# All opening loads on one queue, three x tiles in one transfer, half copies, and two units ahead of a fold

## The chip, the cores and the metric

The kernel runs on one core of a Trainium2 chip. The metric is the device time of one execution in microseconds (us). Before the change it was 225.01 us, the median of three runs (224.81 to 225.06).

A core has five engines that run side by side: TensorE (PE: matmuls and transposes into PSUM; PEld is its weight load), VectorE (DVE), ScalarE (ACT), GpSimd (POOL) and SyncE (SP), which here only issues transfers (DMA). Each engine works its own instructions in program order and waits on semaphores for the others.

## The reference

The input x is 2048 tokens of 512 values. It is normalised per token, and two branches of the result are added to x:

```
xn = (x - mean) / sqrt(var + 1e-5)
A:  q, k, v = split(xn @ wqkv), 32 heads of 16
    pq, pk  = q @ w_phi, k @ w_phi                       (per head, 16 x 16)
    phi(p)  = concat(softmax(p), softmax(-p))
    kv = sum over tokens of phi(pk) v;  z = sum of phi(pk)
    o  = phi(pq) kv / (phi(pq) z + 1e-6);   A = o @ wo
B:  B  = ((xn @ w_gate) * (xn @ w_up)) @ w_down          (1792 wide)
out = x + A + B
```

All data are bf16.

## The kernel before, in words

Tokens are handled in 16 tiles of 128 and in four groups of four tiles (512 tokens). Most of the time is matmuls of the B branch and of the projections. The order on TensorE, VectorE, ScalarE, GpSimd and SyncE is the order of the program: the scheduler is switched off for them (`manual_schedule`), so each engine works what the source issues to it, in that order.

Loads. `dma_x` loads a range of x tiles, `dma_cols` a range of columns of a weight. SyncE issues x tile 0, x tile 1, x tiles 2 and 3, then wk, the first 256 columns of gate and up, w_phi, the next 640 columns of gate and up, x tiles 4 to 7, the last 896 columns of gate and up, x tiles 8 to 15, w_down and wo. The load of wv is issued by ScalarE, behind its first activation in the program (line 96), which is there to load the table for Exp. A token's row of x is 1 KB; a partition's rows of neighbouring tiles are contiguous, so tiles 1 to 3 together are 3 KB per partition.

Normalisation of the first four tiles. On VectorE, for each tile n: `ln_sums` (bn_stats, L146), then `first_apply(n - 1)` (L162), which normalises the tile before, then bn_aggr (L338) and the add of epsilon (L155); GpSimd raises it to the power -0.5 (L157). The last application follows the loop. So tile 0 is normalised only after the statistics of tile 1. Later groups are normalised by `ln_block`, which puts pieces of work ("chores") on a list; they are taken from the list at places set in the program. Their application runs on ScalarE, and their transposes are DMAs from SyncE.

Transposes of the first tiles. `lt(n)` transposes a normalised tile in four matmuls against the identity (L207) and copies the result from PSUM to xnT on ScalarE (L208). `vproj(n)` is the projection with wv in four matmuls (L235), two before and two after the call given as `amid`, by which the next tile's `lt` comes into its middle; the copy to vt is on ScalarE for tile 0, on VectorE for tiles 1 to 3.

wk. w_phi acts on k directly after the projection, so both are folded to one matrix W1k: `wk_transposes(jp)` transposes half of wk (L222) and copies it on ScalarE (L223), `make_bd` spreads w_phi over a block-diagonal on GpSimd (L214), and `fold` multiplies them (L229) and copies to W1k on ScalarE (L231). `kproj(n)` uses W1k and needs all of it.

Units. `ffn(1)` is one unit of the B branch: 128 of the 1792 columns for one group of 512 tokens. It has four gate matmuls (L272), four up matmuls (L276), a copy of gate on ScalarE (L279) and the product on VectorE (L280). There are 56 units, 14 per group; the first one needs the transposes of all four first tiles, and columns 0 to 127 of gate and up.

`warm_up(k)` issues k matmuls on zeros, whose result nobody reads: ten at the start and two between `lt(0)` and `vproj(0)`. PSUM results go through a ring of six banks (`bank`).

Of the kernel before, what the change touches and what calls it, by code (L numbers as in the profile page):

```python
# [9 lines left out]
F32 = mybir.dt.float32  # L10
AF = mybir.ActivationFunctionType
ALU = mybir.AluOpType
# [9 lines left out]
def kernel(  # L22
# [12 lines left out]
    nc = tc.nc  # L35
    P = 128
    S, D = A_x.shape[-2], A_x.shape[-1]
# [4 lines left out]
    DC = D // P  # L42
    FC = F // P
    EPS = 1e-5
    GT = 4
# [12 lines left out]
    wv = wpool.tile([P, DC, D], BF16)  # L58
# [10 lines left out]
    def dma_x(lo, hi):  # L69
        nc.sync.dma_start(out=xall[:, lo:hi, :], in_=x_view[:, lo:hi, :])  # L70

    def dma_cols(eng, w, src, lo, hi, at=0):
        eng.dma_start(out=w[:, :, lo - at:hi - at], in_=src[:, lo:hi].rearrange("(c p) f -> p c f", p=P))

    F1, F2 = 2 * P, 7 * P
    for lo, hi in ((0, 1), (1, 2), (2, 4)):
        dma_x(lo, hi)
    dma_cols(nc.sync, wk, A_wqkv, D, 2 * D, at=D)
    dma_cols(nc.sync, wg, B_w_gate, 0, F1)
    dma_cols(nc.sync, wu, B_w_up, 0, F1)  # L80
# [13 lines left out]
    nc.vector.memset(zeros[:], 0.0)  # L94
    first = consts.tile([P, 1], BF16)
    nc.scalar.activation(out=first[:], in_=zeros[:, 0:1], func=AF.Exp, scale=1.0)
    dma_cols(nc.scalar, wv, A_wqkv, 2 * D, 3 * D, at=2 * D)
    ident = consts.tile([P, P], BF16)
    make_identity(nc, ident[:])
    mhalf = consts.tile([P, GT], F32)  # L100
# [15 lines left out]
    xnT = xpool.tile([P, DC, S], BF16)  # L116
# [16 lines left out]
    lnpool = ctx.enter_context(tc.tile_pool(name="ln", bufs=2))  # L133
# [16 lines left out]
        stats = ln_sums(n)  # L150
        nc.vector.bn_aggr(out=mv, in_=stats[:])

    def ln_rstd(mv, k):
        ve = lnpool.tile([P, GT], F32, name="ve")
        nc.vector.tensor_scalar(out=ve[:, 0:k], in0=mv[:, 0:k, 1], scalar1=EPS, scalar2=None, op0=ALU.add)  # L155
        rstd = lnpool.tile([P, GT], F32, name="rstd", bufs=GT)
        nc.gpsimd.tensor_tensor(out=rstd[:, 0:k], in0=ve[:, 0:k], in1=mhalf[:, 0:k], op=ALU.pow)  # L157
        return rstd
# [18 lines left out]
    def ln_block(lo):  # L177
        mv = mv_tile()
        nb = lnpool.tile([P, GT], F32, name="nb", bufs=GT)
        rstd = []  # L180

        def scales():
            ve = lnpool.tile([P, GT], F32, name="ve4")
            nc.gpsimd.tensor_scalar(out=ve[:], in0=mv[:, :, 1], scalar1=EPS, scalar2=None, op0=ALU.add)
            r = lnpool.tile([P, GT], F32, name="rstd4", bufs=GT)
            nc.gpsimd.tensor_tensor(out=r[:], in0=ve[:], in1=mhalf[:], op=ALU.pow)
            nm = lnpool.tile([P, GT], F32, name="nm")
            nc.gpsimd.tensor_scalar(out=nm[:], in0=mv[:, :, 0], scalar1=-1.0, scalar2=None, op0=ALU.mult)
            nc.gpsimd.tensor_tensor(out=nb[:], in0=nm[:], in1=r[:], op=ALU.mult)
            rstd.append(r)  # L190

        def apply(i):
            xn = xnpool.tile([P, D], BF16, name="xn")
            nc.scalar.activation(out=xn[:], in_=xall[:, lo + i, :], func=AF.Identity,
                                 scale=rstd[0][:, i:i + 1], bias=nb[:, i:i + 1])
            nc.sync.dma_start(out=xnT[:, :, (lo + i) * P:(lo + i + 1) * P], in_=xn[:], transpose=True)

        for i in range(GT):
            chores.append(lambda i=i: ln_stats(lo + i, mv[:, i, :]))
        chores.append(scales)  # L200
        for i in range(GT):
            chores.append(lambda i=i: apply(i))

    def lt(n):
        tp = bank("tp", BF16).rearrange("p (c t) -> p c t", c=DC)
        for c in range(DC):
            nc.tensor.transpose(out=tp[:, c, :], in_=xns[n][:, c * P:(c + 1) * P], identity=ident[:])  # L207
        nc.scalar.copy(out=xnT[:, :, n * P:(n + 1) * P], in_=tp)  # L208

    bd = consts.tile([P, DC, 8, DH], BF16)  # L210

# [51 lines left out]
    def ffn(k):  # L263
        for _ in range(k):
            if not units:
                return
            T, f = units.pop(0)
            if f == 0:
                hTs[T] = hpool.tile([P, FC, TT], BF16, name="hT", tag="h")
            gps = bank("g")  # L270
            for c in range(DC):
                nc.tensor.matmul(gps, lhsT=wg[:, c, f * P:(f + 1) * P], rhs=xnT[:, c, T * TT:(T + 1) * TT],  # L272
                                 start=(c == 0), stop=(c == DC - 1))
            ups = bank("u")
            for c in range(DC):
                nc.tensor.matmul(ups, lhsT=wu[:, c, f * P:(f + 1) * P], rhs=xnT[:, c, T * TT:(T + 1) * TT],  # L276
                                 start=(c == 0), stop=(c == DC - 1))
            g_sb = gpool.tile([P, TT], BF16, name="g_sb")
            nc.scalar.copy(out=g_sb[:], in_=gps)  # L279
            nc.vector.tensor_tensor(out=hTs[T][:, f, :], in0=ups, in1=g_sb[:], op=ALU.mult)  # L280
# [19 lines left out]
    def warm_up(k):  # L300
        for _ in range(k):
            nc.tensor.matmul(warm, lhsT=zeros[:, 0:P], rhs=zeros[:], start=True, stop=True)
# [3 lines left out]
    with tc.tile_pool(name="ps_k", bufs=1, space=PSUM) as ps_k:  # L306
        kvps = [ps_k.tile([P, 4, 4, E1], F32, name=f"kv{b}") for b in range(2)]
        phiks = {}

        def vproj(n, copy=nc.scalar.copy, amid=None):  # L310
            ps = bank("pv")
            proj(ps, n, wv, range(2))
            if amid is not None:
                amid()
            proj(ps, n, wv, range(2, DC))
            copy(out=vts[n % NV][:, :, :, 0:DH], in_=ps.rearrange("p (a b c) -> p a b c", a=8, b=4))  # L316

        def kproj(n):
            phiks[n] = features(n, W1k, "k")

        def kv(n):
            vt, phik = vts[n % NV], phiks[n]
            for gr in range(NG):
                nc.tensor.matmul(kvps[gr // 4][:, gr % 4, :, :].rearrange("p a b -> p (a b)"),  # L324
                                 lhsT=phik[:, gr, :], rhs=vt[:, gr, :, :].rearrange("p a b -> p (a b)"),
                                 start=(n == 0 and gr % 4 == 0), stop=(n == NT - 1 and gr % 4 == 3))

        mvs = [mv_tile() for n in range(GT)]
        rstds = []

        def first_apply(n):
            ln_apply(n, mvs[n][:, 0, 0:1], rstds[n][:, 0:1])

        for n in range(GT):
            stats = ln_sums(n)
            if n > 0:
                first_apply(n - 1)
            nc.vector.bn_aggr(out=mvs[n][:, 0, :], in_=stats[:])  # L338
            rstds.append(ln_rstd(mvs[n], 1))
        first_apply(GT - 1)  # L340
        make_bd()
        nc.gpsimd.tensor_tensor(out=M4[:], in0=BO[:, 0:4, :], in1=BO[:, 4:8, :], op=ALU.add)
        lt(0)
        warm_up(2)
        vproj(0, amid=lambda: lt(1))
        vproj(1, copy=nc.vector.tensor_copy, amid=lambda: lt(2))
        wk_transposes(0)
        vproj(2, copy=nc.vector.tensor_copy, amid=lambda: lt(3))
        wk_transposes(1)
        vproj(3, copy=nc.vector.tensor_copy)  # L350
        ffn(1)
        fold(1, W1k, (0, 1))
        ffn(1)
        fold(1, W1k, (2, 3))
        ffn(1)
        ln_block(4)
        ffn(1)
        chore(2)
        kproj(0)
        ffn(1)  # L360
        chore(2)
        ffn(1)
        chore()
        kproj(1)
        ffn(1)
        chore()
        ffn(1)
        kproj(2)
        chore()
        ffn(1)  # L370
        kv(0)
        chore()
        ffn(1)
        kproj(3)
        chore()
        ffn(1)
        kv(1)
        ffn(1)
        nc.sync.dma_start(out=wT2[:, 0, :, :], in_=A_wqkv[:, 0:D], transpose=True)
        for n in range(GT, NT):  # L380
            if n in (4, 8):
                ln_block(n + 4)
            vproj(n)
            kproj(n)
            chore(1 if n % GT < 2 else 0)
            ffn(1)
            kv(n - 2)
            chore((1, 2, 2, 2)[n % GT])
            if n >= 8 and n % 2 == 0:
                qproj((n - 8) // 2)  # L390
            if n == 6:
                fold(0, W1q, (0, 1))
            ffn(1)
            if n == 6:
                fold(0, W1q, (2, 3))
        ffn(1)
        kv(NT - 2)
        ffn(1)
        kv(NT - 1)
        for b in range(2):  # L400
            nc.vector.tensor_tensor(out=KV[:, 4 * b:4 * b + 4, :, :], in0=kvps[b][:],
                                    in1=_bcast_ap(M4[:], [M4[:].ap[0], [0, 4], [E1, 4], [1, E1]]), op=ALU.mult)
        qproj(4)
        ffn(1)
# [64 lines left out]
```

## Time and profile before

| what | value |
|---|---|
| median of three runs | 225.01 us |
| the profiled execution | 224.9 us |
| its span, first to last instruction | 223.2 us |
| TensorE busy | 217.4 us (97%) |
| VectorE busy | 137.9 us (62%) |
| ScalarE busy | 90.3 us (40%) |
| GpSimd busy | 72.1 us (32%) |
| moved by DMA | 19.91 MB, mean 89 GB/s |

The profile is one execution. Times in its views count from the first instruction. The chain of waits follows what ended last backwards, at each step to what released it; its lines give the start, the length and the engine with the line of the program. A line of the timeline gives the start, the length, the engine and line, the operation with what it writes and reads, how often it is repeated there, and in square brackets how long the engine was idle before it and what released it. A line for a load gives the issuing queue, how many there are, the size of each and the median time from issue to landing. An idle engine costs nothing unless the chain runs through it.

### The profile page before, as it was taken

Reading aid. Unit: us, or ns where it says so; the run is one execution under the profiler, and the core shown is the slowest. Engines: PE = TensorE matmul, PEld = TensorE weight load, DVE = VectorE, ACT = ScalarE, POOL = GpSimd, SP = SyncE. Lnnn points to the kernel's source line nnn. Section 1 sums busy time; section 2 is a strip of 40 time slices with the busy share of each in tenths; the row PEclk is TensorE's granted clock in tenths of the full one; section 3 lists DMA queues with packets and bytes.
Section 4 is the critical chain, followed back from the end, with each engine's and each line's share of the span. In section 5 each row is a group of like instructions: output and inputs, shape, how many; then the busy total and the mean of one; then the engine's idle time right before and its main releaser. Section 6 shows DMA issues by size and latency. Waiting matters only on the chain.

```text
span 223.2 us, 3437 instructions
## 1 busy us (share of the span) xinstructions
PE 217.4 (97%) x1278; PEld 105.4 (47%) x1278; DVE 137.9 (62%) x237; ACT 90.3 (40%) x161; POOL 72.1 (32%) x59
## 2 busy tenths in 40 slices
PE   7799999999999999999999999999999999999994
PEld 2354444445444444444454444444444444444453
DVE  5634986586559875757679975097745746444321
ACT  2574575448955685646354122222222222100000
POOL 3310455336235663636315453014033033000000
PEclk9999999999999999999999999999999999999999
DMA  6999923501110224020203664314431431622301
GB/s 178 317 381 394 349 55 74 94 1 21 38 38 0 47 50 94 1 47 3 47 1 71 99 140 94 75 24 94 94 73 24 93 72 24 91 55 71 72 25 47
DMA packets 44481, 19.91 MB, mean 89 GB/s; under 512 B 35248, under 2 KB 44080, under 8 KB 44336
## 3 DMA queue, kind: packets, MB, share of 16 engines
q1 hardware_dynamic: 43936, 19.16, 34.8%
q10 hardware_dynamic: 528, 0.52, 0.8%
q8 instruction: 10, 0.16, 0.3%
q14 instruction: 7, 0.06, 0.1%
HBM read 9.19 MB, written 2.10 MB: 51 GB/s over the span
## 4 chain that ended last, share of the span: by engine, by line
PE 95%; DMA 2%; DVE 1%; SPq 0%; ACT 0%; issue 0%
PE fin L288 22%; PE u L276 22%; PE g L272 22%; PE fin L291 6%; PE k L235 6%; PE q L235 6%; PE pv L235 6%; DMA xall<-in_A_x_dram 2%; PE ab L412 2%; PE kv L324 2%; PE pq L229 1%; PE tp L222 0%; PE tp L207 0%; SPq L70 0%; DVE stats L146 0%; ACT xnT L208 0%
## 5 line engine op out<-in xcount | busy, mean ns | idle before, releaser
L276 PE MATMUL u<-xnT,wu 128*128 128x512 bf16 x224 | 57.5, 379 | 0.0
L272 PE MATMUL g<-xnT,wg 128*128 128x512 bf16 x224 | 57.5, 379 | 0.0
L280 DVE TENSOR_TENSOR hT<-u,g_sb 128x512 bf16<-128x512 f32 x56 | 37.1, 668 | 28.3 <-PE u L276 19.5
L247 DVE TENSOR_REDUCE sums<-e 128x64 f32<-128x1024 f32 x32 | 38.9, 1215 | 21.5 <-ACT e L244 21.5
L279 ACT CAST g_sb<-g 128x512 bf16<-128x512 f32 x56 | 32.9, 588 | 46.5 <-PE g L272 46.5
L288 PE MATMUL fin<-wd,hT 128*128 128x512 bf16 (+1 forms) x238 | 51.1, 366 | 0.0
L251 POOL TENSOR_TENSOR phiq<-e,rs 128x1024 bf16<-128x1024 f32 x16 | 30.9, 1932 | 61.5 <-DVE rs L249 53.2
L251 POOL TENSOR_TENSOR phik<-e,rs 128x1024 bf16<-128x1024 f32 x16 | 30.9, 1932 | 47.6 <-DVE rs L249 45.6
L276 PEld LDWEIGHTS <-wu 128*128 128x128 bf16 x224 | 21.9, 98 | 26.4
L288 PEld LDWEIGHTS <-hT 128*128 128x128 bf16 x238 | 23.0, 98 | 24.1
L272 PEld LDWEIGHTS <-wg 128*128 128x128 bf16 x224 | 21.1, 98 | 23.4
L235 PEld LDWEIGHTS <-xnT 128*128 128x128 bf16 x192 | 17.2, 97 | 18.7 <-ACT xnT L208 1.7
L294 DVE TENSOR_TENSOR o_sb<-fin,xall 128x512 bf16<-128x512 f32 (+1 forms) x17 | 11.2, 656 | 22.4 <-PE fin L291 22.4
L243 ACT ACTIVATE e<-q 128x512 f32<-128x512 f32 x16 | 9.5, 596 | 26.1 <-PE q L235 26.1
L249 DVE RECIPROCAL rs<-sums 128x64 f32<-128x64 f32 x32 | 17.7, 553 | 3.1
L235 PE MATMUL pv<-wv,xnT 128*128 128x512 bf16 x64 | 16.9, 379 | 0.6 <-ACT xnT L208 0.5
L291 PE MATMUL fin<-wo,oT 128*128 128x512 bf16 (+1 forms) x68 | 16.6, 366 | 0.0
L235 PE MATMUL k<-W1k,xnT 128*128 128x512 bf16 x64 | 16.4, 379 | 0.0
L235 PE MATMUL q<-W1q,xnT 128*128 128x512 bf16 x64 | 16.4, 378 | 0.0
L243 ACT ACTIVATE e<-k 128x512 f32<-128x512 f32 x16 | 9.6, 597 | 7.0 <-PE k L235 7.0
L316 ACT CAST vt<-pv 128x512 bf16<-128x512 f32 x13 | 7.7, 591 | 11.5 <-PE pv L235 11.5
L146 DVE BATCH_NORM_STATS2 stats<-xall 128x6 f32<-128x512 bf16 x16 | 10.7, 670 | 2.2 <-DMA xall<-in_A_x_dram 2.2
(50 smaller groups left out, 125.1 us busy)
## 6 DMA issues: line engine op xcount, KB each, us to landing
out_dram<-o_sb SPq DMA_DIRECT2D x15, 128.0 KB, 1.9
wd<-in_B_w_down_dram SPq DMA_DIRECT2D x1, 1792.0 KB, 17.5
xall<-in_A_x_dram SPq DMA_DIRECT2D x1, 1024.0 KB, 13.4
wg<-in_B_w_gate_dram SPq DMA_DIRECT2D x1, 896.0 KB, 8.5
wu<-in_B_w_up_dram SPq DMA_DIRECT2D x1, 896.0 KB, 11.4
wg<-in_B_w_gate_dram SPq DMA_DIRECT2D x1, 640.0 KB, 7.9
wu<-in_B_w_up_dram SPq DMA_DIRECT2D x1, 640.0 KB, 7.0
wv<-in_A_wqkv_dram ACTq DMA_DIRECT2D x1, 512.0 KB, 4.4
```

What stands on the lines that cost most here:

```text
L235: nc.tensor.matmul(ps, lhsT=xnT[:, j, n * P:(n + 1) * P], rhs=w[:, j, :], start=(j == 0), stop=(j == DC - 1))
L243: nc.scalar.activation(out=e[:, :, 0, :], in_=pfv, func=AF.Exp, scale=1.0)
L247: nc.vector.tensor_reduce(out=sums[:], in_=ev, axis=AX.X, op=ALU.add)
L249: nc.vector.reciprocal(out=rs[:].rearrange("p a b -> p (a b)"), in_=sums[:])
L251: nc.gpsimd.tensor_tensor(out=phi[:].rearrange("p g (x f) -> p (g x) f", f=DH), in0=ev, in1=rs[:].to_broadcast((P, 2 * H, DH)), op=ALU.mult)
L272: nc.tensor.matmul(gps, lhsT=wg[:, c, f * P:(f + 1) * P], rhs=xnT[:, c, T * TT:(T + 1) * TT], start=(c == 0), stop=(c == DC - 1))
L276: nc.tensor.matmul(ups, lhsT=wu[:, c, f * P:(f + 1) * P], rhs=xnT[:, c, T * TT:(T + 1) * TT], start=(c == 0), stop=(c == DC - 1))
L279: nc.scalar.copy(out=g_sb[:], in_=gps)
L280: nc.vector.tensor_tensor(out=hTs[T][:, f, :], in0=ups, in1=g_sb[:], op=ALU.mult)
L288: nc.tensor.matmul(ps, lhsT=hTs[T][:, f, t4 * P:(t4 + 1) * P], rhs=wd[:, f, lo:lo + w], start=(f == 0), stop=False)
L291: nc.tensor.matmul(ps, lhsT=oTs[n][:, c, :], rhs=wo[:, c, lo:lo + w], start=False, stop=(c == DC - 1))
L294: nc.vector.tensor_tensor(out=o_sb[:], in0=ps, in1=xall[:, n, lo:lo + w], op=ALU.add)
```

## The change

The loads of the opening are all issued by SyncE, in this order: x tile 0; x tiles 1 to 3 in one transfer; wv; then wk and the rest as before. ScalarE issues none. The copies of the transposes of tiles 0 and 1 are made in two halves of two column blocks each. The two warm-up matmuls between `lt(0)` and `vproj(0)` are left out; the ten at the start stay. In front of the first fold stand two units instead of one, between the folds one as before, and after the second fold one instead of two, so that four stand in front of the first k projection as before. `ln_rstd` takes the engine of its add as an argument and serves the later groups too; the instructions and their engines are the same, but the later groups now share the buffers `ve` and `rstd` with the first tiles.

```diff
     F1, F2 = 2 * P, 7 * P
-    for lo, hi in ((0, 1), (1, 2), (2, 4)):
-        dma_x(lo, hi)
+    dma_x(0, 1)
+    dma_x(1, 4)
+    dma_cols(nc.sync, wv, A_wqkv, 2 * D, 3 * D, at=2 * D)
     dma_cols(nc.sync, wk, A_wqkv, D, 2 * D, at=D)
...
     nc.scalar.activation(out=first[:], in_=zeros[:, 0:1], func=AF.Exp, scale=1.0)
-    dma_cols(nc.scalar, wv, A_wqkv, 2 * D, 3 * D, at=2 * D)
...
-    def ln_rstd(mv, k):
+    def ln_rstd(eng, mv, k):
         ve = lnpool.tile([P, GT], F32, name="ve")
-        nc.vector.tensor_scalar(out=ve[:, 0:k], in0=mv[:, 0:k, 1], scalar1=EPS, scalar2=None, op0=ALU.add)
+        eng.tensor_scalar(out=ve[:, 0:k], in0=mv[:, 0:k, 1], scalar1=EPS, scalar2=None, op0=ALU.add)
...
         def scales():
-            ve = lnpool.tile([P, GT], F32, name="ve4")
-            nc.gpsimd.tensor_scalar(out=ve[:], in0=mv[:, :, 1], scalar1=EPS, scalar2=None, op0=ALU.add)
-            r = lnpool.tile([P, GT], F32, name="rstd4", bufs=GT)
-            nc.gpsimd.tensor_tensor(out=r[:], in0=ve[:], in1=mhalf[:], op=ALU.pow)
+            r = ln_rstd(nc.gpsimd, mv, GT)
...
-    def lt(n):
+    def lt(n, parts=1):
         tp = bank("tp", BF16).rearrange("p (c t) -> p c t", c=DC)
         for c in range(DC):
             nc.tensor.transpose(out=tp[:, c, :], in_=xns[n][:, c * P:(c + 1) * P], identity=ident[:])
-        nc.scalar.copy(out=xnT[:, :, n * P:(n + 1) * P], in_=tp)
+        for c in range(0, DC, DC // parts):
+            nc.scalar.copy(out=xnT[:, c:c + DC // parts, n * P:(n + 1) * P], in_=tp[:, c:c + DC // parts, :])
...
-            rstds.append(ln_rstd(mvs[n], 1))
+            rstds.append(ln_rstd(nc.vector, mvs[n], 1))
...
-        lt(0)
-        warm_up(2)
-        vproj(0, amid=lambda: lt(1))
+        lt(0, parts=2)
+        vproj(0, amid=lambda: lt(1, parts=2))
...
-        ffn(1)
+        ffn(2)
         fold(1, W1k, (0, 1))
         ffn(1)
         fold(1, W1k, (2, 3))
-        ffn(1)
         ln_block(4)
         ffn(1)
         chore(2)
```

## The prediction

> **What bounds the kernel now.** I read the page's busy line and chain summary first, then the chain of waits for the first 16 us, then the timeline of the same stretch, then the loads.
>
> ```profile
> PE 217.4 (97%) x1278; PEld 105.4 (47%) x1278; DVE 137.9 (62%) x237; ACT 90.3 (40%) x161; POOL 72.1 (32%) x59
> ...
> PE 95%; DMA 2%; DVE 1%; SPq 0%; ACT 0%; issue 0%
> ```
>
> TensorE is busy 97% of the span and carries 95% of the chain. What is left sits in the opening and in the short tail. From the first unit on, pieces of TensorE follow each other without a hole (the eight matmuls of a unit take 2 x 0.86 us), so an opening that ends earlier by some amount ends the kernel earlier by that amount. The chain in the opening (columns: start, length, what):
>
> ```profile
> 1.71 4.88 DMA xall<-in_A_x_dram
> 6.59 0.02 issue
> 6.61 0.69 DVE stats L146
> 7.31 0.33 DVE xn L162
> 7.63 0.05 issue
> 7.68 0.41 PE tp L207 x4
> 8.09 0.02 issue
> 8.11 0.59 ACT xnT L208
> 8.71 0.05 issue
> 8.75 0.60 PE pv L235 x2
> 9.36 0.22 PE tp L207 x4
> ...
> 12.05 1.04 PE pv L235 x4
> 13.09 0.86 PE g L272 x4
> ```
>
> One transfer, x tiles 2 and 3 together, lands at 6.59. Behind it VectorE takes tile 2's statistics, only then applies tile 1's normalisation, and TensorE can transpose tile 1. From 8.75 TensorE is nearly gapless up to the first unit at 13.09: 4.34 us. So the opening is set by a load, by VectorE's order, and by one ScalarE copy. The timeline, same stretch:
>
> ```profile
> 1.22 0.46 ACTq L73 DMA_DIRECT2D wv<-in_A_wqkv_dram  x1
> ...
> 2.99 0.69 DVE L146 BATCH_NORM_STATS2 stats<-xall 128x6 f32<-128x512 bf16 x1 [1.11 <-DMA xall<-in_A_x_dram]
> ...
> 4.01 0.68 DVE L146 BATCH_NORM_STATS2 stats<-xall 128x6 f32<-128x512 bf16 x1
> ...
> 7.22 0.40 DVE L162 TENSOR_SCALAR xn<-xall,mv,rstd 128x512 bf16<-128x512 bf16 x1
> ...
> 8.56 0.41 DVE L162 TENSOR_SCALAR xn<-xall,mv,rstd 128x512 bf16<-128x512 bf16 x1
> ```
>
> And the loads (last column: us from issue to landing):
>
> ```profile
> wv<-in_A_wqkv_dram ACTq DMA_DIRECT2D x1, 512.0 KB, 4.4
> wk<-in_A_wqkv_dram SPq DMA_DIRECT2D x1, 512.0 KB, 6.3
> xall<-in_A_x_dram SPq DMA_DIRECT2D x2, 128.0 KB, 2.3
> xall<-in_A_x_dram SPq DMA_DIRECT2D x1, 256.0 KB, 4.9
> ```
>
> wv, issued on ScalarE's queue at 1.22, landed at 5.62. The 256 KB of x, issued at 1.71, came after it although they are half as large: in this trace a load goes by its issue time over both queues, and wv stood in front of tiles 2 and 3.
>
> **The change, part by part.** I write L for the landing of x tiles 1 to 3 and V for that of wv.
>
> Issue slots. SP issues x tile 0 at 0.79, the next at 1.25, the third at 1.71, wk at 2.18. Afterwards tiles 1 to 3 have the second slot, wv the third (each 0.40 to 0.46 us), and wk keeps 2.18. ScalarE loses an issue of 0.46 us that lay beside its table load (0.78 to 2.06): nothing gained. wk and all behind it have the same 1024 KB in front as before, so I leave their landings: wk 2.18 + 6.3 = 8.5, gate 9.35, up 10.4, w_phi 10.7, and so on. wv's 512 KB now stand in SP's queue too, and SP's own stall (a 2.64 us issue at 4.45) may begin sooner; the loads it holds have margins, given below.
>
> L. Issue at 1.25. Before, 256 KB of x had landed by 1.25 + 2.3 = 3.55, and 768 KB (x 0, x 1, wv) by 5.62. Tiles 0 to 3 are 512 KB, half-way: 4.6. From below, VectorE is busy with tile 0 until about 4.0, so landing before that is worth nothing more. From above, L's 384 KB are no slower than wv's 512 KB, 4.4 us from issue: 5.65. I take the half-way value, 4.6: it comes from loads of the same stretch on both sides.
>
> The fit of the Trainium skill ("DMA: Bandwidth & Descriptors", section "Anatomy of one DMA — SWDGE (gpsimd) path") is 2.0 us plus bytes at 436 GB/s, stated for loads that GpSimd issues; it gives an estimate of 1.25 + 2.0 + 0.9 = 4.15 for L. It fits the 128 KB loads here (2.3 us) and fails for the 256 KB one (4.9 us against 2.6), which had others in front. By it, and by L alone, the end would be 0.45 us earlier than by the rows, 223.7 us; I stay with the rows.
>
> V. With wv last of the same 1024 KB: 768 KB at 5.62, 1024 KB at 6.59 before. That is the value for no faster transfer, and 1.71 + 4.4 = 6.1 the one for its own time from issue. I take 6.4, a little nearer to the first, which counts bytes.
>
> VectorE's path. The new wait: tile 1's statistics started at 4.01 without waiting, now at L + 0.02, and the application of tile 0, which is queued behind them, with them. Before, 6.61 to 7.22 is statistics to application (0.61), and two applications stand 1.34 us apart (7.22, 8.56). So tile 0 is applied at L + 0.63 = 5.23 instead of 4.79 (0.44 us late), tile 1 at L + 1.97 = 6.57 instead of 7.22, tile 2 at L + 3.31 = 7.91 instead of 8.56. There are now three tiles behind the late landing instead of two: 1.34 us of the 1.99 us by which the landing is earlier (6.59 - 4.6) are spent again.
>
> Tile 1 to the first unit. Application 0.41 and 0.05 issue, transposes 0.41, 0.02, then the copy. A whole copy (128x512) is 0.586 us and one of 128x1024 is 1.012: 0.426 per 512 columns on 0.16 fixed, so a half is 0.37, an estimate between 0.20 (the 128x1 activation at 2.08) and 0.586. The first two matmuls read the first half alone: 0.22 us gained. 0.05 more, and tile 1's wv matmuls start at L + 1.97 + 0.46 + 0.43 + 0.37 + 0.05 = L + 3.28. Two halves take 0.74 instead of 0.586 on ScalarE; the second half is read only after the next tile's transposes, which hide that 0.16. From these matmuls to the first unit, 4.34 us as before: L + 7.62. Tile 2's transposes there begin 0.61 after, L + 3.89, and tile 2 is ready at L + 3.31 + 0.41 + 0.05 = L + 3.77: hidden, with 0.1 to spare. With L = 4.6 the first unit starts at 12.22, not 13.09: 0.87 earlier.
>
> The other input. The first wv matmuls start at V + 0.05, and tile 0's first half is there at 5.23 + 0.46 + 0.43 + 0.37 + 0.05 = 6.54, so with V = 6.4 neither waits on the other. By V alone: 0.43 for two matmuls, 0.41 tile 1's transposes, 0.44 half copy with its two hand-overs, then 4.34: V + 5.67 = 12.07, short of 12.22. Both inputs limit within 0.15 us.
>
> Two warm-up matmuls go (0.59 us busy from 5.49): before, the wv matmuls behind them started at 6.33, released by the copy, so nothing was lost to them and nothing is won. What they covered was a hole of TensorE; the holes now are from 5.14 to 5.7 and from 6.1 to 6.54, no longer than the 0.74 before 7.68, across which the page's slices show a granted clock of nine tenths or more. I cost it at 0; if the clock fell, see the rivals.
>
> Two units in front of the fold. Same matmuls, other order; before, TensorE had no hole from first unit to the first k projection (13.09 to 20.89 is four units of 1.73 and two folds of 0.45), so at best 0. What it costs if cover fails: gate and up's second part land at 12.4 and 14.1, wanted by the third unit at 12.22 + 3.45 + 0.45 = 16.1; w_phi's product with the mask is done at 11.86, wanted at 15.6; the last W1k copy ends 1.5 us after its fold starts (14.65 to 16.15), while one unit and the fold, 2.18, stand before the k projection. wk lands 8.5, wanted at L + 3.89 + 0.22 + 0.43 = 9.1: the thinnest margin, 0.6. The helper that now serves both normalisations issues the same GpSimd instructions; the buffers shared were read long before: 0.
>
> Sum. The opening ends 0.87 earlier, everything else is 0. The profiled execution took 224.9 with a span of 223.2 (1.7 around it), 0.1 under the median 225.01. Its forecast is 224.0, the median's 224.1.
>
> **The rivals.**
>
> Tiles 1 to 3 late, slower. All of tile 0's work now hangs on the 384 KB. Break-even is L + 7.62 = 13.09, L = 5.47, and from there each us costs one. The bound from wv's row, 5.65, gives 225.2; the 4.9 us of the 256 KB row, counted from 1.25, is L = 6.15 and 225.7. For it: the trace moved 197 to 252 GB/s in the half-us slices from 2.0 to 3.5 us, against 351 to 366 from 10 to 12 us. Against: in the 4.9 us row wv stood in front, and it no longer does.
>
> wv late. V + 5.67 = 13.09 is V = 7.42: no gain. For it: wv is now last of 1024 KB. At 6.59 the gain is 0.83 and only from 6.97 on is it under 0.45. Time 224.6 to 225.0.
>
> The gain is given back. One of the margins above fails (wk's 0.6, or the W1k copies' 0.7) or the clock falls where the warm-up stood, and the first k projection stands where it stood: 225.0. Against: the loads behind have the same bytes ahead of them. A clock at half over the whole gapless stretch (3.3 us of TensorE work from 8.75 to 12.05) would double that and make 226.5; no row hints at it.
>
> **How the numbers follow.** Forecast, gain over 0.45: 0.74. wv late: 0.12, of which 0.02 still faster. Given back: 0.04, within 0.2% (0.45 us, about what a measurement of this kernel can tell from no change), and 0.01 for the clock, slower. Tiles 1 to 3 late: 0.09, slower. So faster 0.76, no change 0.14, slower 0.10. Range: downward, L at 4.0 and V at its present 5.62 would start the first unit at 11.6, gain 1.5: 223.5; I end at 223.6. Upward to the no-gain cases and a little of the late landing: 225.1.
>
> **What would show it.** Right: the second statistics start near 4.6, waiting for x; tile 1's wv matmuls near 7.9; the first unit near 12.2 and the first k projection near 20.0, with no hole between; half copies of 0.37; GpSimd's w_phi product still near 11. Wrong: statistics after 5.4, wv's first matmuls waiting for a DMA past 6.9, a hole in front of wk's transposes, or matmuls at twice their pitch after 5 us.

## The result: slower in the median, and in two groups

With the change, the kernel takes 226.21 us (median of 20 executions, 224.63 to 226.86) against 225.05 us before (median of 20, 224.81 to 225.45). The ratio of the two is 1.0037, with a 95% interval of 1.0023 to 1.0050: slower, where I had forecast 224.1.

The executions do not scatter evenly. Seven took 224.63 to 225.18, thirteen 225.96 to 226.86, and none lies between. Of the thirteen, ten have a mean granted TensorE clock of 0.992, the others and all seven of the lower group 1.000. The profiled execution of the change is one of the upper group: 226.68 us, span 224.9. Its page has the granted clock in 40 slices:

```profile
PEclk9799999999999999999999999999999999999999
```

The second slice, 5.6 to 11.2 us, holds 7 tenths where the kernel before had 9. The chain of waits of the changed kernel for the first 20 us (start, length, what), against the one shown of before:

```profile
1.25 4.46 DMA xall<-in_A_x_dram
5.71 0.02 issue
5.73 0.69 DVE stats L146
6.43 0.32 DVE xn L162
6.75 0.05 issue
6.80 0.41 PE tp L204 x4
7.21 0.02 issue
7.23 0.38 ACT xnT L206
7.61 0.04 issue
7.66 0.61 PE pv L233 x2
8.26 0.30 PE tp L204 x4
8.56 1.71 PE pv L233 x4
10.27 0.43 PE tp L204 x4
...
14.83 0.86 PE g L270 x4
```

The first unit (line g) starts at 14.83; before it was 13.09. That is 1.74 later, and the profiled executions differ by 226.68 - 224.9 = 1.78, so all but 0.04 us of the loss is in the opening. Two things stand in these lines. x tiles 1 to 3 land at 5.71, not at the 4.6 that I had taken. And from 8.43 on the matmuls take twice their time: four wv matmuls 1.71 us where two took 0.43, four transposes 0.43 instead of 0.22. The loads of the changed kernel (last column: us from issue to landing):

```profile
wv<-in_A_wqkv_dram SPq DMA_DIRECT2D x1, 512.0 KB, 5.6
wk<-in_A_wqkv_dram SPq DMA_DIRECT2D x1, 512.0 KB, 6.6
...
xall<-in_A_x_dram SPq DMA_DIRECT2D x1, 384.0 KB, 4.5
```

wv, issued at 1.71, lands at 7.3 instead of 6.4. The clock can be read from the busy time by stretches (columns: stretch, its length, then the busy time and the number of instructions of TensorE, its weight load, VectorE, ScalarE and GpSimd, then granted clock, DMA share, GB/s). First the changed kernel, from the instant at which its clock was raised (the records of the clock begin there):

```profile
5.02:8.43 3.41, 1.57 (x13) 0.61 (x12) 2.55 (x9) 0.65 (x2) 0.56 (x1) 1.00 1.08 348
8.43:11.85 3.42, 3.42 (x18) 1.73 (x16) 1.89 (x6) 1.82 (x4) 1.88 (x3) 0.50 1.12 307
```

and the kernel before, from the rise of the clock in its own trace:

```profile
4.45:7.86 3.41, 2.30 (x15) 0.73 (x14) 2.11 (x9) 0.59 (x1) 0.86 (x2) 1.00 0.99 322
```

In the changed kernel TensorE worked 1.57 us in the 3.41 us after the rise, and for the next 3.41 us the clock was 0.50. Before it worked 2.30 us, and the clock stayed.

By my own path, L + 7.62 with L = 5.71 gives 13.33: 0.24 of the 1.74 us is the landing, and the other 1.50 us I put down to the clock. The row of the fallen clock allows that much: 3.42 us of TensorE work at half the clock are 1.71 us at the full one.

### The profile page after: what moved, and what is told of

Its sections match the earlier page's. It is cut to its first block, busy times and chain, and to the rows that moved or that the text cites. A ratio compares the mean times of both kernels' runs of the same rounds, so it can differ in the third digit from the quotient of the medians.

```text
span 224.9 us, 3411 instructions
## 1 busy us (share of the span) xinstructions
PE 217.4 (97%) x1252; PEld 106.1 (47%) x1276; DVE 137.9 (61%) x237; ACT 90.6 (40%) x163; POOL 72.2 (32%) x59
## 4 chain that ended last, share of the span: by engine, by line
PE 95%; DMA 2%; issue 1%; DVE 1%; SPq 0%; ACT 0%
PE g L270 22%; PE u L274 21%; PE fin L286 21%; PE pv L233 7%; PE fin L289 6%; PE k L233 6%; PE q L233 6%; DMA xall<-in_A_x_dram 2%; PE kv L322 2%; PE ab L408 2%; PE pq L227 1%; PE tp L204 1%; PE tp L220 0%; DVE stats L146 0%; DVE o_sb L292 0%
## 5 line engine op out<-in xcount | busy, mean ns | idle before, releaser
L292 DVE TENSOR_TENSOR o_sb<-fin,xall 128x512 bf16<-128x512 f32 (+1 forms) x17 | 11.2, 656 | 22.4 <-PE fin L289 21.5
L233 PE MATMUL pv<-wv,xnT 128*128 128x512 bf16 x61 | 17.8, 404 | 0.6 <-ACT xnT L206 0.5
```

What stands on the lines that cost most here:

```text
L233: nc.tensor.matmul(ps, lhsT=xnT[:, j, n * P:(n + 1) * P], rhs=w[:, j, :], start=(j == 0), stop=(j == DC - 1))
L292: nc.vector.tensor_tensor(out=o_sb[:], in0=ps, in1=xall[:, n, lo:lo + w], op=ALU.add)
```

## The experiments

Two theories to begin with. Clock theory: the late landing and the two missing warm-ups leave TensorE with too little work after the ten warm-ups, and the clock falls. Landing theory: the late x tiles are the whole loss. All kernels were compared with the kernel before on the same chip, whose medians were 224.99 to 225.12 there. A hole is a time in which TensorE is idle.

**Warm-ups put back.** In the changed kernel:

```diff
         lt(0, parts=2)
+        warm_up(2)
         vproj(0, amid=lambda: lt(1, parts=2))
```

> The changed kernel with the two warm-up matmuls put back in front of tile 0's wv projection. In the profile of the changed kernel TensorE worked for about 1.6 us of the 3.4 us from 5.0 to 8.4, and the granted clock then fell to 0.50 for 3.4 us. Clock theory (too little TensorE work after the ten warm-ups lets the clock fall): the two add about 0.4 us there; if that is enough the clock stays at 1.00 and every execution takes 224.6 to 225.2; if not, the times scatter as before. Landing theory (the late landing of x tiles 1 to 3 is the whole loss): 226.2 as with the change, whatever the clock does.

225.04 us (224.74 to 226.42, 12 executions), ratio 0.9998 [0.9986, 1.0011]. Ten executions took 224.74 to 225.13, two 226.34 and 226.42. So the two matmuls bring most executions back, though x still lands late (5.41 in the profiled one): the landing is not the whole loss. The profiled execution was one of the two. Its clock did not fall after a rise, it rose late, only at 10.45. Chain of waits of this kernel:

```profile
6.50 0.61 PE tp L204 x4
7.10 0.85 PE warm L300 x2
7.96 0.85 PE pv L233 x2
8.81 0.43 PE tp L204 x4
9.24 1.53 PE pv L233 x4
10.76 0.22 PE tp L204 x4
```

Transposes at 0.43 for four until 10.45, at 0.22 afterwards. The mean clock of this execution is given as 1.000 all the same, since the records begin with the rise; that may be why three slow executions of the change have 1.000 too.

**Sixteen warm-ups at the start instead of ten.**

```diff
-    warm_up(10)
+    warm_up(16)
```

> The changed kernel with sixteen warm-ups at the start instead of ten, which end at about 6.5 at the full clock's pitch, before tile 0's transposes at 6.8, so that they delay nothing. Clock theory: no fall of the clock, first unit near 13.1 instead of 14.8, 224.7 to 225.1, no execution near 226.5. Landing theory: 226.2, since x tiles 1 to 3 still land at 5.7.

225.41 us (224.84 to 225.91), 1.0007 [0.9998, 1.0016]. No execution near 226.5: the clock theory's main point holds. But the time is above the expected 224.7 to 225.1. The chain of waits says why:

```profile
1.24 6.21 PE warm L300 x16
7.45 0.24 PE tp L204 x4
```

The clock rose only at 6.51 here, the warm-ups before it had half the pace, and tile 0's transposes, whose input was there at about 6.3 (x landed at 5.24), waited for the last of them until 7.3. I had priced all six additional ones at the full pace.

**x tile 1 in a transfer of its own.**

```diff
-    dma_x(0, 1)
-    dma_x(1, 4)
+    for lo, hi in ((0, 1), (1, 2), (2, 4)):
+        dma_x(lo, hi)
```

> The changed kernel with x tile 1 and x tiles 2 and 3 loaded in two transfers again, wv behind them on SyncE. Landing theory: tile 1 lands near 3.6, tile 0 is applied at 4.8, tiles 2 and 3 land near 4.6 and wv near 6.5; then wv limits, first unit near 12.2, 224.2. Clock theory alone: the hole of TensorE after the warm-ups is shorter (tile 0's transposes at 5.2), work from 5.0 to 8.4 is over 2 us, the clock stays at 1.00 and the time is 224.2 to 224.9. If one transfer of 3 KB rows lands no later than two, the time is that of the change, 224.6 to 226.9.

225.60 us, 1.0012 [0.9987, 1.0038]: unclear, as the times again fall in two groups, five of 224.29 to 224.66 and one of 225.19, six of 226.01 to 227.25. Tile 1 landed at 3.63 and tile 0 was transposed at 5.37, as expected; but tiles 2 and 3 landed at 5.45 instead of 4.6, and wv took TensorE's place as the one waited for:

```profile
2.18 5.44 DMA wv<-in_A_wqkv_dram
7.62 0.04 issue
7.66 1.01 PE pv L233 x2
```

TensorE was idle for 1.90 us in front of wv, worked 1.34 us in the 3.42 us after the rise of the clock (3.94 to 7.36), and the clock fell. Both parts of what I expected of the clock were wrong for this run: work there was not over 2 us, since I had put wv at 6.5. The five of the lower group, 0.5 to 0.8 us under the kernel before, show what the early tile is worth where the clock holds. And 512 KB of x are down at 5.45 in two transfers as at 5.2 to 5.7 in one: the one large transfer is not what makes them late.

**wv back on ScalarE's queue.**

```diff
-    dma_cols(nc.sync, wv, A_wqkv, 2 * D, 3 * D, at=2 * D)
...
     nc.scalar.activation(out=first[:], in_=zeros[:, 0:1], func=AF.Exp, scale=1.0)
+    dma_cols(nc.scalar, wv, A_wqkv, 2 * D, 3 * D, at=2 * D)
```

> The changed kernel with wv issued by ScalarE again, at 1.22, beside x tiles 1 to 3 at 1.25. If loads go by their issue time over both queues, wv lands near 5.6 and x tiles 1 to 3 near 6.6 or later: 0.9 us later than with the change, first unit near 14 at the full clock, and a still longer hole on TensorE, so a fallen clock in most executions: 226 to 227.5. If the two queues share, x lands near 5.7 and the time is that of the change, 224.6 to 226.9.

227.00 us (225.84 to 227.93), 1.0080 [1.0059, 1.0100], inside the first expectation's range of times, but not by its mechanism: x tiles 1 to 3 landed at 6.17 and wv after them at 7.76. So two loads issued together on two queues need not land as those of before did, where I had read an order by issue time. The long hole in front of tile 0 was there (TensorE 1.43 us in the 3.41 us from 5.75), and the clock fell.

**The kernel before without its two warm-ups.**

```diff
         lt(0)
-        warm_up(2)
         vproj(0, amid=lambda: lt(1))
```

> The kernel before without the two warm-up matmuls between tile 0's transposes and its wv projection, all else as before. The granted clock goes by stretches of 3.4 us: stretches with 1.34, 1.43 and 1.57 us of TensorE work were followed by a clock of 0.50 (three kernels with x tiles 1 to 3 or wv late), one with 2.30 us was not (the kernel before). Without the two, the one of the kernel before holds about 1.9. Clock theory: if 1.9 is enough, 225.05 in every execution, the two matmuls alone are not the cause and the longer hole in front of tile 0 is; if not, a part of the executions stands 1.2 to 1.8 above, near 226.5. As I predicted it: 225.05 always.

225.04 us (224.87 to 226.26), 1.0010 [0.9998, 1.0023]. Nine executions of 12 took 224.87 to 225.14, three 225.94 to 226.26. The profiled one is of the three:

```profile
4.33:7.74 3.41, 1.75 (x10) 0.46 (x8) 1.86 (x6) 0.59 (x1) 0.97 (x2) 1.00 1.02 317
7.74:11.15 3.41, 3.20 (x14) 1.57 (x15) 2.06 (x8) 1.59 (x3) 1.56 (x3) 0.50 1.13 306
```

So the kernel before stands near the edge: without 0.43 us of useless work, a quarter of its executions fall into an upper group, and the one of them that was profiled lost its clock. One of the 29 executions of the kernel before itself on this chip took 226.04 too; it was not profiled. With the change it is thirteen of twenty, with a longer hole in front of tile 0.

**Two transfers for x and four warm-ups.** The changed kernel with x tile 1 by itself, as above, and `warm_up(4)` between `lt(0, parts=2)` and `vproj(0, ...)`.

> The changed kernel with x tile 1 and x tiles 2 and 3 in two transfers, wv behind them on SyncE, and four warm-ups between tile 0's transposes and its wv projection, where TensorE waits for wv. Clock theory: no executions near 226.3; all take what the undisturbed ones of the same loads without warm-ups took, 224.3 to 224.7. If the scatter comes from the loads and not from the clock, it stays: 224.3 to 227.2. If wv is early the four cost up to 0.4: 224.8.

224.78 us, 0.9989 [0.9977, 1.0001]; ten executions of 224.48 to 225.09 and one of 225.84. With the same loads the upper group is gone but for that one execution, which was not profiled: the scatter came with the clock and not with the loads. The time is 0.1 above what was expected; in the profiled execution the four began just before the rise of the clock at 6.21 and ended at 7.09, where wv had landed (7.05).

**wv on SyncE in the kernel before.**

```diff
-    for lo, hi in ((0, 1), (1, 2), (2, 4)):
-        dma_x(lo, hi)
+    dma_x(0, 1)
+    dma_x(1, 2)
+    dma_cols(nc.sync, wv, A_wqkv, 2 * D, 3 * D, at=2 * D)
+    dma_x(2, 4)
...
-    dma_cols(nc.scalar, wv, A_wqkv, 2 * D, 3 * D, at=2 * D)
```

> The kernel before with wv issued by SyncE, between x tile 1 and x tiles 2 and 3, so that the order of the loads is the one in which they landed before; everything else as before, the two warm-ups too. If only the order of issue counts (as I predicted), x tiles 2 and 3 land at 6.6 and the time is 225.05. If loads of one queue are served more slowly in the first microseconds than the same loads on two queues, x tiles 2 and 3 land at 7.0 to 7.6 as the last of 1024 KB did with all on SyncE: 225.5 to 226.1.

226.03 us (225.65 to 226.30), 1.0044 [1.0031, 1.0057], in one group. The order of landing is that of the kernel before, and still x tiles 2 and 3 are a microsecond later:

```profile
2.18 5.57 DMA xall<-in_A_x_dram
7.75 0.02 issue
7.77 0.69 DVE stats L147
```

So the same order and the same bytes in front did not bring the same landing. Of the 1.16 us between the two profiled executions 0.47 is the issue, 2.18 instead of 1.71; from there to landing it took 5.6 us instead of 4.9. In the profiled executions of the other kernels with the loads of before it took 5.2 to 5.5, so between 0.1 and 0.7 us are left to the one queue.

This trace also narrows down what makes the clock fall. The late tile left a hole of 1.41 us, longer than the change's 1.38, and the clock held, with 1.96 us of TensorE work in the second stretch after its rise at 4.21:

```profile
8.84 0.40 PE L208 MATMUL tp<-ident,xn 128*128 128x128 bf16 x4 [1.41 <-DVE xn L163]
...
7.62:11.04 3.42, 1.96 (x15) 0.99 (x16) 2.51 (x8) 1.34 (x3) 1.10 (x2) 1.00 1.14 312
```

In the kernel before without its two warm-ups the longest hole up to the fall was 1.02 us, and yet the clock fell. So the longest hole does not tell the two cases apart; the sum of the work in a stretch does, with the limit between 1.75 and 1.96 us of 3.41 in these two traces.

**Two queues, x first.** From the kernel with four warm-ups:

```diff
-    def dma_x(lo, hi):
-        nc.sync.dma_start(out=xall[:, lo:hi, :], in_=x_view[:, lo:hi, :])
+    def dma_x(lo, hi, eng=nc.sync):
+        eng.dma_start(out=xall[:, lo:hi, :], in_=x_view[:, lo:hi, :])
...
-    for lo, hi in ((0, 1), (1, 2), (2, 4)):
-        dma_x(lo, hi)
-    dma_cols(nc.sync, wv, A_wqkv, 2 * D, 3 * D, at=2 * D)
+    dma_x(0, 1)
+    dma_x(1, 2, nc.scalar)
+    dma_x(2, 4)
+    dma_cols(nc.scalar, wv, A_wqkv, 2 * D, 3 * D, at=2 * D)
```

> The changed kernel with the opening loads on two queues in another order: SyncE issues x tile 0, then x tiles 2 and 3, ScalarE x tile 1, then wv; and four warm-ups between tile 0's transposes and its wv projection. Queue theory (two queues are served faster in the first microseconds than one): x tile 1 lands near 3.5, x tiles 2 and 3 near 4.6, wv near 6.2, 0.9 earlier than with all on SyncE; first unit near 12, 223.9 to 224.3, and the clock does not fall. If the bytes alone count, wv lands near 7.0 as the last of 1024 KB does on one queue, and the time is that of the same kernel with all on SyncE, 224.5 to 225.1. If ScalarE's early issue delays its table load, no loss: its first copy is at 6.

225.09 us (224.92 to 225.27), 1.0002 [0.9993, 1.0011]. The queue theory falls: wv landed at 7.7 (6.5 us from its issue at 1.22), later than the 7.05 on one queue, and tile 0 itself only at 3.92 instead of 3.06:

```profile
0.79 3.13 DMA xall<-in_A_x_dram
3.92 0.02 issue
3.94 0.70 DVE stats L147
```

Tile 1 was issued beside tile 0 here, but that this made tile 0 late is not shown: in two kernels with the loads of before tile 0 landed at 3.7 and 3.8 as well.

What the late kernels had in common was then x itself: 512 KB of x are down at 5.2 or later in all of them, whatever queue and whatever size of transfer. That led to the next one.

**The halves alone, and the units in front of the fold alone**, each put into the kernel before as the change has it.

> The kernel before with the copies of tiles 0 and 1 in halves alone. Half a copy took 0.38 in the profile of the changed kernel, a whole one 0.59 before: tile 1's wv matmuls start 0.2 earlier, 8.55 instead of 8.75, and the first unit with them: 224.85. If the second half's later end holds something up: 225.05. TensorE's work in the stretch after the warm-ups stays the same, so no fall of the clock.

> The kernel before with two units in front of wk's first fold, one between the folds and one behind, as in the change, and nothing else. TensorE had no hole there before, and the margins that I counted (0.7 us for W1k, over 2 us for the loads) hold: 225.05, within 0.1. If W1k's copies come too late for the first k projection, or a transfer is wanted too early: 225.3 to 226.

Halves: 224.92 us, 0.9995 [0.9987, 1.0004], no more than 0.1 gained and not told from nothing. Units first: 225.07 us, 1.0003 [0.9994, 1.0012], nothing, as predicted.

**Another numbering of the tokens.** A tile was every sixteenth token; here it is 128 neighbours, for the input and the output alike, so that its rows lie together in memory.

```diff
-    x_view = A_x.flatten_outer_dims().rearrange("(p n) d -> p n d", n=NT)
-    out_view = out.flatten_outer_dims().rearrange("(p n) d -> p n d", n=NT)
+    x_view = A_x.flatten_outer_dims().rearrange("(n p) d -> p n d", n=NT)
+    out_view = out.flatten_outer_dims().rearrange("(n p) d -> p n d", n=NT)
```

First in the changed kernel with its two warm-ups put back, then in the one with two x transfers and four warm-ups:

> The changed kernel with the two warm-ups put back, and with another numbering of the tokens: a tile is 128 neighbouring tokens, for x and for the output, so a tile's 128 KB lie together in memory instead of 1 KB out of every 16 KB. The result is the same. Stride theory: x tiles 1 to 3 land at 5.2 to 5.7 in four kernels because rows 16 KB apart are read slowly; now they land near 4.6, where the count of bytes put them, and the executions that keep their clock take 224.0 to 224.4 instead of 224.7 to 225.1. Start theory (everything is slow in the first microseconds of loading, whatever it reads): 5.2 to 5.7 again and 224.7 to 225.1. If rows of 1 KB instead of 3 KB cost more than the stride: later than 5.7, 225.2 and more.

> The kernel with x tile 1 and x tiles 2 and 3 in two transfers, wv behind them on SyncE and four warm-ups in front of the wv projection, with the same other numbering of the tokens. Its time before was 224.78 (224.48 to 225.1 but for one). Stride theory: wv, which limits it, lands near 6.5 instead of 7.05, 224.1 to 224.5. Start theory: wv lands at 7.0 again and 224.5 to 225.1.

224.28 us (224.07 to 224.44), 0.9964 [0.9952, 0.9976], and 224.11 us (223.67 to 224.68), 0.9961 [0.9949, 0.9974]: both clearly under the kernel before, both times as the stride theory has it. Loads of the first of the two:

```profile
wv<-in_A_wqkv_dram SPq DMA_DIRECT2D x1, 512.0 KB, 4.6
...
xall<-in_A_x_dram SPq DMA_DIRECT2D x1, 384.0 KB, 3.3
```

The 384 KB land at 4.56 instead of 5.41, wv at 6.3 instead of 7.0; they are the same bytes, now in rows of 1 KB. In the second kernel wv lands at 6.63 instead of 7.05, tile 1 at 3.21 instead of 3.70, but tiles 2 and 3 only 0.14 earlier (5.12 and 5.26), which the stride theory does not explain. The landings are compared by one execution each.

Two questions were left: does the numbering act elsewhere in the kernel, and is the fall of the clock the late landing's doing, or that of the two missing warm-ups? So it was put into the kernel before alone, and into the change as it stands.

> The kernel before with the other numbering of the tokens (a tile's 128 KB together in memory) and nothing else. If the numbering acts through the landing of the first x tiles alone: x tiles 2 and 3 land a little earlier, 6.2 to 6.5 instead of 6.6 to 7.2, the time is 224.6 to 225.0, and the change with the same numbering stays 0.4 or more below it. If it acts elsewhere (the later x loads, the output's stores), the kernel before gains the same 0.8 as the others: 224.2 to 224.4.

> The changed kernel as it stands, without the two warm-ups, with the other numbering of the tokens. x tiles 1 to 3 then land near 4.6 and TensorE's hole in front of tile 0 is 0.9 us shorter. Clock theory: about 2.3 us of TensorE work in the 3.4 us after the warm-ups, as in the kernel before, and no fall of the clock: 224.0 to 224.4, which is what I predicted for the change. If the missing two warm-ups alone make the clock fall, part of the executions stands near 225.8.

The kernel before gains nothing: 225.00 us, 0.9999 [0.9990, 1.0007]. Its x tiles 2 and 3 still landed at 6.71:

```profile
1.71 5.00 DMA xall<-in_A_x_dram
6.71 0.02 issue
6.74 0.69 DVE stats L146
```

There they stand behind wv, and nothing else that sets the time becomes faster by the numbering. The change with it takes 224.13 us (223.94 to 224.69, five executions), 0.9964 [0.9950, 0.9977], and none of them stands near 225.8 or above, without the two warm-ups. Five executions are enough to tell this from the thirteen of twenty of the change, but too few to tell it from the quarter that was slow in the kernel before without the two. In the profiled one TensorE worked 2.85 us in the 3.41 us after the rise, and x tiles 1 to 3 landed at 4.36. This execution, one of the two at 224.69, also shows what came next:

```profile
4.95:8.36 3.41, 2.85 (x20) 0.98 (x19) 3.17 (x12) 1.75 (x5) 1.12 (x2) 1.00 0.99 311
...
2.23 7.36 DMA wk<-in_A_wqkv_dram
9.59 0.05 issue
9.64 0.62 PE tp L220 x8
...
12.89 0.86 PE g L270 x4
```

wk came at 9.59 where it is wanted at 9.1 or sooner: the thinnest of the margins that I had listed. In the two earlier kernels with the new numbering wk landed at 8.6 and 8.3.

## Why the prediction was wrong

By its own steps:

- **L, the landing of x tiles 1 to 3: mis-sized.** I took 4.6, between 256 KB of x at 3.55 and 768 KB of x and wv at 5.62, with 5.65 as the upper bound. Measured with these loads: 5.71, 5.41 and 5.24. The interpolation treated x and wv as bytes of one kind. With the rows of a tile together in memory the same step measured 4.56 and 4.36, and the time was 224.28 and 224.13, against my 224.1. So the path behind L was right and its first term was not. The slower-going rival, tiles 1 to 3 late, had the break-even at 5.47, and the three landings lie on both sides of it; it accounts for +0.24 us in the profiled execution. The lower group, 224.63 to 225.18, lies around the time before as such landings would have it, but none of it was profiled.
- **V, wv's landing: mis-sized.** 6.4 against 7.27, 6.98 and 6.95: 0.55 to 0.87 us late, behind x tiles that were 0.64 to 1.11 us late. In the profiled execution of the change this cost nothing, as the first wv matmuls waited for a copy until 7.66. That a load goes by its issue time over both queues, and lands as before with the same bytes in front, was read from one trace and did not hold in the runs that changed a queue.
- **The two warm-ups at 0: wrong, and the main loss.** I compared the longest hole with one of 0.74 us before and concluded that the clock would stand. With L late the hole in front of tile 0 was 1.38 us and not 0.56; and what decides is visible only over a whole stretch of 3.41 us: the clock stayed with 1.96, 2.30 and 2.85 us of TensorE work and fell after 1.34, 1.43, 1.57 and 1.75. It cost 1.50 us in the profiled execution, by the path. Neither half of the cause does it alone to this extent: 2 of 12 executions were in an upper group with the late landing and the two warm-ups, 3 of 12 with the landing of before and without them, 13 of 20 with both against it. I had the fallen clock as a rival at 1 in 100 with "no row hints at it". The row with 2.30 of 3.41, in which the two warm-ups were a fifth of the work, could have been asked for; how near it is to the limit only the runs showed. The 226.5 of that rival is close to the measured time by luck: its own terms, 3.3 us of work at half the clock on top of 224.1, make 227.4 at least, and the fallen clock lasted one stretch of 3.41 us. The Trainium skill ("TensorE: Matmul & The Clock Gate", Part 1) lets the clock halve after at least one idle window of about 3.4 us, with windows that run freely; the steps of 3.41 us at changing instants agree with that, the idle window does not: no hole in these openings was longer than 1.90 us, so by that sentence the change would have lost nothing, and the measurement decides.
- **VectorE's path, the length of a half copy, the way to the first unit: right.** Tile 0 was applied at L + 0.63 (6.34 with L = 5.71). Tile 1's wv matmuls were to start at L + 3.28 = 8.99; in the trace their first weight load is at 9.02, and the matmul waits until 9.21 for the one before it, at half the clock. A half copy took 0.38 against 0.37. At the full clock the first unit came at L + 7.75 with the other numbering (12.31, L = 4.56), against 7.62; there the warm-ups were still in the way until 5.69 and again until 6.65. What the halves are worth by themselves was not told from nothing (0.9995 [0.9987, 1.0004]).
- **Two units in front of the fold at 0: right**, 1.0003 [0.9994, 1.0012].
- **The estimate worked out from the Trainium skill ("DMA: Bandwidth & Descriptors", section "Anatomy of one DMA — SWDGE (gpsimd) path"), 4.15 for L**, was further off than the rows with the loads of the change; with the other numbering L was 4.36 and 4.56, between it and the 4.6 of the rows.
- **Given back later: wk's margin of 0.6** was the next one to fail, in one profiled execution whose opening was early enough to reach it (L = 4.36).

## What to carry to other kernels

Before taking useless matmuls out of an opening, or putting a later load in front of its first tile, sum TensorE's busy time over the stretch of the clock's own length after the rise, not the longest hole: here 1.96 us of 3.41 held and 1.75 did not, in one trace each, and the loss (1.5 us) was larger than anything that the opening had to give. Price a load by loads of the same layout: the same 384 KB took about a microsecond longer in strided rows than in neighbouring ones. And where the times of a kernel fall into two groups, explain the groups before the median.

## What the runs showed of the hardware

- The granted clock moves in steps of 3.41 us that begin at a different instant in each execution: the rise came at 3.94, 4.21, 4.33, 4.45, 5.02, 5.75, 6.21, 6.51 and 10.45 us in kernels that all began their warm-ups at 1.24. That one kernel falls into either group fits this; no kernel was profiled in both. A stretch with 2.60 us of (slow) TensorE work, 3.62 to 7.03 in the kernel with its warm-ups put back, did not raise it; one with 2.70 did (0.52 to 3.94, with x in two transfers).
- 384 KB of x in rows 16 KB apart landed 4.0 to 4.5 us after issue with wv behind it on its own queue, in neighbouring rows 3.1 to 3.3. In the traces such a load lands in 16 parts: the first of them was down at 4.08 to 4.14 us with either numbering, the last at 5.24 to 5.71 with rows 16 KB apart and at 4.36 to 4.56 with neighbouring rows. For the 256 KB of x tiles 2 and 3 alone there was no such difference (3.5 and 3.4 us). Which part of the way to memory makes the difference was not tried, and the stride is not parted from the length of the rows, which went from 3 KB to 1 KB.
- Open: why two queues did not help when x was first (wv at 7.7 us) and whether x tiles 2 and 3, which took 5.6 us from issue behind wv on one queue and 4.9 to 5.5 behind it on two, are really slower there.
- What is faster than the kernel before and the change is the change with the other numbering of the tokens, 224.13 us, or with two x transfers and four warm-ups besides, 224.11 us; the runs do not tell the two apart.
